# First five attention steps written in another order: inverse sums leave ahead of the transposes, operands split one step sooner, one more piece of w_in converted

## The chip, the core and the metric

The kernel runs on one core of a Trainium2 chip. The metric is the device time of one execution in microseconds (us). A core has a matrix engine (PE, its weight loads shown as PEld), a vector engine (DVE), a scalar engine (ACT), a general engine (POOL) and a queue engine (SP), which here issues every transfer. Each engine runs its own instruction list in order and waits on semaphores for the others; the transfers of SP's queue start in the order written, each once its own waits are over.

## The reference, cut to what matters

Three layers follow one another, on 4 batches of 576 tokens:

```
scores = q k^T / 8 ; cum = cumsum(max(s, 0)) ; scores += min(-(cum_i - cum_j), 0), causal
attn   = exp(scores - max) / (sum + 1e-9) ;  x = attn v          # 4 x 8 heads of 64
h = gelu(x w_in) ; u, v = halves of h ; v = layernorm(v) g_ln
x = x + (u * (w_sg v + b_sg)) w_out                              # w_in and other weights are float64
theta = x w_theta ; y = w_tok_r (x cos theta) + w_tok_i (x sin theta)
out = (x + y) + max((x + y) w_ch, 0)
```

## The kernel before

Attention works on 16 pairs of heads, one step p for each. All matrix products are split into high and low parts: `kh` is K rounded by ACT, `kl` the rest by POOL, `qh` Q/8 rounded by POOL, `ql` the rest by DVE. A step holds, for its pair p: `scores(p, 0)` and `scores(p, 1)` on PE (tiles `sc`, two groups of row blocks that share the same PSUM banks); `reduced` on DVE (adds the bias `C`, takes minimum and maximum, writes `E` and `negm`); `expo` on ACT (exponential, with row sums `sm`); and, for the pair before, `inverse` (DVE: `sm` + 1e-9, then the reciprocal into `r`), seven groups of transposes of `E` on PE (tiles `T`, copied to `Ef` and `E0` by ACT and DVE), and `load_r`. For the pair two before, `values` multiplies by v (tiles `Y`, `Z`), and DVE multiplies the result with `xT`, which holds the inverse sums.

The inverse sums travel: `r` is transposed on PE into a tile `T`, ACT copies it to `rT`, SP stores that to `rd` in HBM, and `load_r` loads `rd` back, spread over partitions, as `xT`. SP cannot issue that load before the store has landed, and whatever stands behind the load in SP's queue waits with it.

The float64 weight `w_in` comes in 8 pieces: `load_piece(k)` (SP, into one of two buffers `wraw`), `scale(k)` (ACT, `wtab` from `wraw`), `bits(k)` (three DVE instructions on `wtab`), `part32(k)` (ACT `wih`, POOL `wil`). A buffer is free for piece k+2 after `bits(k)`.

Up to step 4 (`FIXED = 5`) the order on every engine is the order in which the program text is written (`fixed()` chains it). From step 5 on a scheduler orders the instructions and weaves the first layer after attention (`ffn`, tiles `fo`) into the steps; there the table `PLAN` says which piece is converted (C) or loaded (L) at which of a step's four places (G, H, B: the same for `w_sg` and two vectors). The first half of `ffn_in` needs the pieces 0 to 3, the second half (`fo<-x,wih`) the pieces 4 to 7.

Of the kernel before, what the change touches and what calls it, by code (L numbers as in the profile page):

```python
# [9 lines left out]
F32 = mybir.dt.float32  # L10
# [4 lines left out]
ALU = mybir.AluOpType  # L15
# [24 lines left out]
HALF = [(0, 288), (288, 288)]  # L40
# [15 lines left out]
class Kernel:  # L56
# [12 lines left out]

    PLAN = {5: ("C4 L6", "C5 L7", "C6 G0", "C7 G1 B"), 6: ("H0 G2", "H1 G3", "H2 G4", "H3 G5"),  # L70
# [102 lines left out]
    def begin(self, es):  # L173

        nc = self.nc
        c = self.cp
        p = self.pool(es, "cum")
# [57 lines left out]
        cpos = p.tile([32, S], F32, name="cpos")  # L235
# [3 lines left out]
        os = []  # L239
# [10 lines left out]
        def part(i):  # L250
            a, n = HALF[i]
            cs = slice(a, a + n)
            nc.scalar.copy(ch[:, cs], os[i][0:32, 0:n])
            nc.vector.tensor_copy(cpos[:, cs], os[i][0:32, 0:n])
            nc.sync.dma_start(self.cd[:, cs], cpos[:, cs])
            nc.vector.tensor_tensor(cl[:, cs], cpos[:, cs], f32(ch[:, cs]), op=ALU.subtract)

        def spread(i, j):

            a, n = HALF[i]  # L260
            cs = slice(a, a + n)
            o = ps.tile([P, 512], F32, name="spread", **(
                dict(tag="spread", bufs=2) if i == 0 else dict(tag=f"cumo{HALF[j][0]}")))
# [9 lines left out]
        self.split_k()  # L273
        for f in copies:
            f()
        self.scores(0, 0)
        for j in (0, 1):
            spread(1, j)()
        self.load_pair(1)

# [14 lines left out]
    def attention_pools(self, es):  # L295
# [130 lines left out]
    def transposes(self, pr, kind, j, pool=None):  # L426
# [12 lines left out]
        if kind == "a" and not j:  # L439
            nc.tensor.transpose(T[:, 256:384], self.st[pr % 2][1], self.ident)  # L440
        if kind != "d":
# [4 lines left out]
        def away():  # L446
            if kind == "b":
                nc.vector.tensor_copy(Ef[:, 512:1024], T)  # L448
            elif kind == "c":
                nc.scalar.copy(Ef[:, 0:512], T)  # L450
            elif kind == "d":
                nc.vector.tensor_copy(E0[:, 0:512], T)
            else:
                nc.scalar.copy(Ef[:, 1024:1280], T[:, 0:256])
                if j == 0:
                    rT = self.a1.tile([10, P], F32, name="rT")
                    nc.scalar.copy(rT, T[0:10, 256:384])
                    nc.sync.dma_start(self.rd[pr].rearrange("j (c n) -> (j c) n", c=5), rT)
                else:
                    nc.scalar.copy(E0[:, 512:576], T[:, 256:320])  # L460
        return away

    def transposed(self, pr):
# [79 lines left out]
    def split_k(self):  # L543
        K = self.raw.pop(("K", 0))
        qh, ql, kh, kl = self.ops[0]
        self.rnd("act", kh, K)
        for a, n in HALF:
            self.sub("pool", kl[:, a:a + n], K[:, a:a + n], kh[:, a:a + n])

    def first_steps(self):  # L550

        nc = self.nc
        one = (0, 1)
        for p in range(self.FIXED):
            V = None
            if p:
                self.scores(p, 0)

            Q, K = self.raw["Q", p + 1], self.raw.pop(("K", p + 1))
            qh, ql, kh, kl = self.operands(p + 1)  # L560
            if p:
                self.load_cum(p + 1)
                self.rnd("act", kh, K)
            nc.gpsimd.tensor_scalar(qh, Q, 0.125, 1.0, op0=ALU.mult, op1=ALU.mult)
            if p == 0:
                self.spin(self.psT.tile([P, 512], F32, name="spin", tag="T"), 8)
            else:
                self.sub("pool", kl, K, kh)
            for j in one:
                self.reduced(p, (1, 0, 4), (j,))  # L570
                self.expo(p, (1, 0, 4), (j,))
                if p == 0 and j == 0:
                    self.rnd("act", kh, K)
                    self.sub("pool", kl, K, kh)
                    self.load_cum(1)
            if p:
                self.inverse(p - 1)
            if p > 1:
                V = self.values(p - 2)
            elif p:  # L580
                self.spin(self.psT.tile([P, 512], F32, name="spin", tag="T"), 10)
            self.split_q(p + 1)
            if p:
                self.scale(p - 1)
            self.load_pair(p + 2, "K")
            self.load_pair(p + 2, "Q")
            self.load_v(p)
            self.scores(p, 1)
            if V:
                V("pool")  # L590
            if p == 0:
                self.load_piece(0)
                for t in (3, 2):
                    self.reduced(0, (t,))
                    self.expo(0, (t,))
                self.aux()
                del self.cums[0]
                self.load_piece(1)
                self.spin(self.psT.tile([P, 512], F32, name="spin", tag="T"), 12)
                continue  # L600
            g = p - 1
            a0 = self.transposes(g, "a", 0)
# [25 lines left out]
        self.inverse(self.FIXED - 1)  # L628

    def attention(self):  # L630
# [466 lines left out]
    def run(self):  # L1097
        nc = self.nc
        with ExitStack() as root, ExitStack() as right2, ExitStack() as left2:
# [10 lines left out]
            with self.fixed():  # L1110
# [11 lines left out]
                self.attention_psum(aps)  # L1122
                self.first_steps()
            with aps:
# [137 lines left out]
```

## Time and profile before

| what | us |
|---|---|
| median of 3 runs (lowest, highest) | 666.54 (666.25, 667.63) |
| the profiled execution, its own time | 668.43 |
| its span, first to last instruction | 666.7 |
| PE busy in the span | 630.3 (95%) |
| DVE, ACT, POOL busy | 427.8, 357.0, 178.5 |

The span is what the trace shows; 1.73 us of the profiled execution lie around it. PE is busy 95% of the span, so the idle time of PE, 36 us in all, and the stretches in which its clock is granted only in part are where time can come from; the rows further down show where they lie. The waits are read from the timeline of an engine, where the bracket behind a row gives how long the engine stood idle ahead of it and what ended that.

### The profile page before, as it was taken

To read this page: it belongs to the slowest core of one execution; us is meant where nothing else is said; L and a number is where in the kernel's file an instruction comes from. 1 tells how busy PE (TensorE), PEld (TensorE's weight loads), DVE (VectorE), ACT (ScalarE), POOL (GpSimd) and SP (SyncE) were. 2 spreads that over 40 slices of the span, in tenths; PEclk is the share of its full clock that TensorE was granted. 3 is DMA by queue.
4 is the path that set the end of the run, shared out by engine and by line. 5 is a ranking of instruction groups with operands and counts; after the bars stand their busy time and mean duration, and the time that the engine had idled before them with its cause. 6 is when DMAs were issued, how large, how long until landed. Compare 5 with 4: busy or idle time off the path is not lost.

```text
span 666.7 us, 12668 instructions
## 1 busy us (share of the span) xinstructions
PE 630.3 (95%) x4719; PEld 551.4 (83%) x4719; DVE 427.8 (64%) x1049; ACT 357.0 (54%) x833; POOL 178.5 (27%) x207
## 2 busy tenths in 40 slices
PE   8888869989999999999997799999999999999997
PEld 6666657768877888778787789899999999989997
DVE  6798567757387563863269977787772577468422
ACT  5876548784587744874265335566550454255100
POOL 4344423333205332044396633120000100100000
PEclk9899898999999999999999889999999999999999
DMA  4677554445632565201355789721002100300101
GB/s 121 213 256 240 161 166 145 122 134 179 222 104 88 154 195 187 69 19 73 137 147 179 248 261 363 250 90 55 1 1 88 56 1 36 107 0 2 72 1 72
DMA packets 49806, 83.57 MB, mean 125 GB/s; under 512 B 7921, under 2 KB 19793, under 8 KB 49745
## 3 DMA queue, kind: packets, MB, share of 16 engines
q1 hardware_dynamic: 49744, 82.76, 38.5%
q8 instruction: 37, 0.61, 0.4%
q14 instruction: 25, 0.20, 0.1%
HBM read 61.61 MB, written 21.13 MB: 124 GB/s over the span
## 4 chain that ended last, share of the span: by engine, by line
PE 66%; DMA 9%; DVE 8%; ACT 7%; POOL 5%; issue 3%; SPq 1%; DVEq 0%; ACTq 0%; POOLq 0%
PE yo L109 17%; PE fo L109 13%; PE th L109 8%; PE co L109 8%; PE wo L109 6%; PE Y L109 5%; PE sc L109 5%; PE T L438 3%; DMA wraw<-in_moe_w_in 3%; ACT E L408 2%; DMA rd<-rT 2%; POOL vT L851 2%; DVE E L397 2%; PE tp L1000 1%; DMA xT<-rd 1%
## 5 line engine op out<-in xcount | busy, mean ns | idle before, releaser
L408 ACT ACTIVATE E<-E,negm 128x192 f32<-128x192 f32 (+4 forms) x160 | 88.2, 553 | 1.7 <-DVE negm L397 1.6
L109 PE MATMUL yo<-wkh,zh 128*128 128x288 f32 x288 | 85.2, 296 | 0.2 <-DVE x2T L1073 0.2
L109 PE MATMUL yo<-wkl,zh 128*128 128x288 f32 x288 | 85.2, 296 | 0.0
L109 PE MATMUL yo<-wkh,zl 128*128 128x288 f32 x288 | 85.2, 296 | 0.0
L397 DVE CUSTOM_DVE_ANT_0 E<-sc,C 128x192 f32<-128x192 f32 (+4 forms) x160 | 68.5, 483 | 6.6 <-PE sc L109 6.4
L438 PE MATMUL T<-ident,E 128*128 128x128 f32 x400 | 57.6, 279 | 13.1 <-DVE xT L500 4.9
L109 PE MATMUL fo<-x,wih 128*128 128x288 f32 x256 | 57.3, 306 | 6.1 <-ACT vT L891 3.7
L438 PEld LDWEIGHTS T<-ident,E 128*128 128x128 f32 x400 | 46.4, 142 | 17.8 <-DVE Ef L448 6.0
L109 PEld LDWEIGHTS yo<-wkh,zh 128*128 128x128 f32 x288 | 54.0, 188 | 0.7 <-DVE x2T L1073 0.4
L109 PEld LDWEIGHTS yo<-wkl,zh 128*128 128x128 f32 x288 | 54.1, 188 | 0.3
L109 PEld LDWEIGHTS yo<-wkh,zl 128*128 128x128 f32 x288 | 54.0, 188 | 0.1
L109 PE MATMUL co<-u,wch 128*128 128x288 f32 x256 | 53.0, 295 | 0.0
L102 POOL TENSOR_SCALAR xt<-x2s 128x128 fp32r<-128x128 f32 x16 | 10.8, 691 | 156.1 <-DVE x2s L106 156.1
L109 PEld LDWEIGHTS fo<-x,wih 128*128 128x128 f32 x256 | 42.1, 189 | 8.6 <-ACT vT L891 3.9
L109 PE MATMUL wo<-gh,woh 128*128 128x288 f32 x128 | 39.2, 309 | 7.0 <-ACT gh L98 3.7
L109 PE MATMUL fo<-wih,x 128*128 128x512 f32 x128 | 43.7, 413 | 0.0
L109 PE MATMUL th<-wth,x2s 128*128 128x512 f32 x128 | 42.9, 400 | 0.0
L448 DVE COPY Ef<-T 128x512 f32<-128x512 f32 x32 | 21.6, 685 | 32.9 <-PE T L438 32.5
L98 ACT CAST u<-x2T 128x576 fp32r<-128x576 f32 x16 | 10.8, 672 | 59.3 <-DVE x2T L1073 59.3
L109 PEld LDWEIGHTS co<-u,wch 128*128 128x128 f32 x256 | 41.6, 188 | 0.0
L109 PE MATMUL sc<-kh,qh 64*128 64x288 f32 (+1 forms) x192 | 39.3, 374 | 0.4
L109 PE MATMUL wo<-gl,woh 128*128 128x288 f32 x128 | 37.7, 308 | 1.3 <-DVE gl L106 1.3
(203 smaller groups left out, 1767.3 us busy)
## 6 DMA issues: line engine op xcount, KB each, us to landing
C<-cd SPq DMA_DIRECT2D x15, 576.0 KB, 4.1
Q<-in_q SPq DMA_DIRECT2D x16, 288.0 KB, 3.4
K<-in_k SPq DMA_DIRECT2D x16, 288.0 KB, 3.4
xT<-rd SPq DMA_DIRECT2D x32, 144.0 KB, 3.2
xd<-xT SPq DMA_DIRECT2D x16, 288.0 KB, 2.1
gd<-uT SPq DMA_DIRECT2D x16, 288.0 KB, 2.1
gr<-gd SPq DMA_DIRECT2D x16, 288.0 KB, 3.5
xr<-xd SPq DMA_DIRECT2D x16, 288.0 KB, 4.2
```

The lines of the kernel that those rows point to most:

```text
L98: nc.scalar.copy(out, src)
L102: nc.gpsimd.tensor_scalar(out, src, 1.0, 1.0, op0=ALU.mult, op1=ALU.mult)
L109: return self.nc.tensor.matmul(out, lhsT, rhs, start=start, stop=stop)
L397: self.nc.vector.tensor_tensor_reduce(at if j else at[:, ::-1], self.sc[t, j].rearrange("p (b k) -> p b k", k=64), C[:, j, 0:n].rearrange( ...
L408: self.nc.scalar.activation(at, at, AF.Exp, bias=self.negm[pr % 2][:, j, c:c + 1], scale=-1.0, accum_out=sm[:, j * 5 + c:j * 5 + c + 1])
L438: nc.tensor.transpose(T[:, col:col + P], E[:, c:c + P], self.ident)
L448: nc.vector.tensor_copy(Ef[:, 512:1024], T)
L851: nc.gpsimd.tensor_scalar(vT[0:r, t], vT[0:r, t], rs[0:r, t:t + 1], nm[0:r, t:t + 1], op0=ALU.mult, op1=ALU.add)
L1000: nc.tensor.transpose(tp[0:r, dt * P:(dt + 1) * P], x2T[:, dt, a:a + r], self.ident)
```

## The change

Seven things are different, all in the first five steps and the text around them:

- The start: `kh`, `qh`, `ql` and `kl` of pair 0 stand ahead of the copies of the cumulated sums (`part`), all four `spread` products stand behind `scores(0, 0)`, and the loads of pair 1 are issued among them.
- `load_piece(0)` and `load_piece(1)` stand in step 0 ahead of the loads of pair 2; piece 0 is converted in step 0, piece p in step p, so pieces 0 to 4 are done in the fixed part and `load_piece` goes up to 6. `PLAN` loses C4 and L6.
- `high(p + 2)` (`qh`, `kh`, `kl`) stands at the end of step p, ahead of `part32(p)`; before, it stood in step p + 1 behind `part32(p)`.
- `inverse(p - 1)` stands between the two halves of `reduced(p, (1, 0, 4))`, and `turned` (transpose of `r`, copy to `rT`, store) ahead of `scores(p, 1)`; before, it was part of the first transposes.
- K(p+2) is loaded before `inverse`, Q(p+2) after `low_q`; `load_v` and `load_cum` stand ahead of them.
- Step 1 has 8 spin products (idle work on PE) instead of 10.
- SP, too, now has to keep its later transfers behind the last one written before `values(3)`.

```diff
-    PLAN = {5: ("C4 L6", "C5 L7", "C6 G0", "C7 G1 B"), ...
+    PLAN = {5: ("C5 L7", "C6", "G0", "C7 G1 B"), ...
...
-        self.split_start()
+        Q, K = self.raw.pop(("Q", 0)), self.raw.pop(("K", 0))
+        qh, ql, kh, kl = self.operands(0)
+        nc.gpsimd.tensor_scalar(qh, Q, 0.125, 1.0, op0=ALU.mult, op1=ALU.mult)
+        self.rnd("act", kh, K)
+        self.low_q(0, Q)
+        self.load_pair(1, "Q")
+        for a, n in HALF:
+            self.sub("pool", kl[:, a:a + n], K[:, a:a + n], kh[:, a:a + n])
         part(0)
-        self.split_q(0)
-        copies = [spread(0, 0), spread(0, 1)]
+        self.load_pair(1, "K")
         part(1)
...
+    def high(self, pr):
+        K = self.raw.pop(("K", pr))
+        qh, ql, kh, kl = self.operands(pr)
+        self.nc.gpsimd.tensor_scalar(qh, self.raw["Q", pr], 0.125, 1.0, op0=ALU.mult, op1=ALU.mult)
         self.rnd("act", kh, K)
+        self.sub("pool", kl, K, kh)
...
+        self.load_piece(0)
+        self.load_cum(1)
...
+        self.load_piece(1)
+        self.load_pair(2, "Q")
+        self.load_pair(2, "K")
+        self.load_v(0)
+        self.scale(0)
...
+        self.bits(0)
+        self.load_piece(2)
+        self.high(2)
+        self.part32(0)
+        self.spin(self.psT.tile([P, 512], F32, name="spin", tag="T"), 12)
+        for p in range(1, self.FIXED):
+            g = p - 1
+            self.scores(p, 0)
+            self.load_cum(p + 1)
+            self.load_v(p)
+            self.load_pair(p + 2, "K")
+            self.reduced(p, (1, 0, 4), (0,))
+            self.expo(p, (1, 0, 4), (0,))
+            self.inverse(g)
+            self.reduced(p, (1, 0, 4), (1,))
+            self.expo(p, (1, 0, 4), (1,))
+            self.low_q(p + 1, self.raw.pop(("Q", p + 1)))
+            self.load_pair(p + 2, "Q")
...
+            self.turned(g, self.psF.tile([P, 512], F32, name="T", tag="fo"))
+            self.scores(p, 1)
             if p > 1:
+                away("pool")
+            self.scale(p)
...
-            self.bits(p - 1)
-            self.part32(p - 1)
-            self.load_piece(p + 1)
+            self.bits(p)
+            self.load_piece(p + 2)
+            if p + 2 <= self.FIXED:
+                self.high(p + 2)
+            self.part32(p)
...
         for e, i in self.ends.items():
-            if e != mybir.EngineType.SP:
-                behind.enter_context(self.tc.issue_after(i))
+            behind.enter_context(self.tc.issue_after(i))
```

SP's queue in step 2 of the kernel before, from the load of `C` for pair 3 to the piece of `w_in` (`rd<-rT` stores the inverse sums of pair 1, `xT<-rd` loads them back):

```order
L324 DMA C_584<-cd_60 128x1152
L320 DMA K_619<-in_k 128x576
L320 DMA Q_621<-in_q 128x576
L335 DMA v02_76<-in_v 64x64 x2
L336 DMA vr_623<-in_v 128x4x128
L514 DMA xd_57<-xT_534 128x576
L458 DMA rd_62<-rT_679 10x128
L477 DMA xT_711<-rd_62 64x576 x2
L704 DMA wraw_278<-in_moe_w_in 128x1024
```

The same stretch now:

```order
L328 DMA C_593<-cd_60 128x1152
L339 DMA v02_76<-in_v 64x64 x2
L340 DMA vr_595<-in_v 128x4x128
L324 DMA K_599<-in_k 128x576
L324 DMA Q_616<-in_q 128x576
L470 DMA rd_62<-rT_634 10x128
L523 DMA xd_57<-xT_540 128x576
L486 DMA xT_718<-rd_62 64x576 x2
L705 DMA wraw_278<-in_moe_w_in 128x1024
```

The store of the inverse sums has moved ahead of the store `xd`, which waits for the result of `values`; K and Q have moved behind v.

DVE in step 2 before: the two halves of `reduced` for the two heads, then `inverse`, then `ql` of the next pair (`negm0_77` alone is the read of an accumulator):

```order
L397 ISA E_579,negm0_77<-sc_543,C_418 128x9x64
L397 ISA negm0_77 128x1
L397 ISA E_579,negm0_77<-sc_544,C_418 128x192
L397 ISA negm0_77 128x1
L397 ISA E_579,negm0_77<-sc_544,C_418 128x64
L397 ISA negm0_77 128x1
L397 ISA E_579,negm0_77<-sc_544,C_418 128x576
L397 ISA negm0_77 128x1
L413 TENSOR_SCALAR sm1_81<-sm1_81 128x10
L414 RECIPROCAL r1_82<-sm1_81 128x10
L541 SCALAR_TENSOR_TENSOR ql_581<-Q_452,qh_580 128x576
```

and now:

```order
L401 ISA E_592,negm0_77<-sc_556,C_428 128x9x64
L401 ISA negm0_77 128x1
L417 TENSOR_SCALAR sm1_81<-sm1_81 128x10
L418 RECIPROCAL r1_82<-sm1_81 128x10
L401 ISA E_592,negm0_77<-sc_557,C_428 128x192
L401 ISA negm0_77 128x1
L401 ISA E_592,negm0_77<-sc_557,C_428 128x64
L401 ISA negm0_77 128x1
L401 ISA E_592,negm0_77<-sc_557,C_428 128x576
L401 ISA negm0_77 128x1
L542 SCALAR_TENSOR_TENSOR ql_548<-Q_451,qh_547 128x576
```

`inverse` has moved ahead of the second head's three reductions. ACT around the end of step 0 before (the `E` rows are exponentials, `sm_79` the sums of step 0):

```order
L408 ACTIVATE E,sm_79<-E,negm_77 128x576
L408 ACTIVATE E,sm_79<-E,negm_77 128x448 x2
L408 ACTIVATE E,sm_79<-E,negm_77 128x320 x2
L98 CAST kh<-K 128x576
L408 ACTIVATE E,sm_81<-E,negm_78 128x192
```

and now (`wtab` is `scale`, `wih` is `part32`):

```order
L412 ACTIVATE E,sm_79<-E,negm_77 128x576
L710 ACTIVATE wtab<-wraw 128x512
L412 ACTIVATE E,sm_79<-E,negm_77 128x448 x2
L412 ACTIVATE E,sm_79<-E,negm_77 128x320 x2
L98 CAST kh<-K 128x576
L98 CAST wih<-wtab 128x512
L412 ACTIVATE E,sm_81<-E,negm_78 128x192
```

`scale(0)` now stands in step 0, between the exponentials of the first and of the second group, and `wih` of piece 0 ahead of step 1's exponentials.

## Rows read from the trace of the kernel before

**Rows 1.** Windows: length, busy PE, PEld, DVE, ACT, POOL, PE clock, DMA share, GB/s.
```profile
17.80:30.00 12.20, 9.88 (x93) 8.11 (x94) 9.69 (x29) 9.40 (x30) 2.70 (x3) 0.86 0.78 244
30.00:41.30 11.30, 10.03 (x106) 7.38 (x108) 9.74 (x31) 8.51 (x28) 5.06 (x6) 1.00 0.71 230
...
52.40:63.80 11.40, 9.68 (x78) 6.12 (x80) 11.07 (x32) 9.29 (x29) 5.71 (x6) 1.00 0.73 225
63.80:70.00 6.20, 3.61 (x52) 2.90 (x48) 0.22 (x2) 0.62 (x1) 1.27 (x1) 1.00 0.78 246
70.00:74.00 4.00, 3.93 (x13) 3.20 (x14) 3.19 (x16) 3.09 (x9) 2.19 (x3) 0.57 0.37 147
...
92.40:105.50 13.10, 8.10 (x47) 6.27 (x47) 9.34 (x29) 9.45 (x24) 2.56 (x2) 0.74 0.21 71
105.50:667.00 561.50, 540.96 (x3968) 484.25 (x3967) 351.81 (x814) 286.82 (x628) 138.54 (x153) 0.99 0.35 114
```

**Rows 2.** Waits of PE up to 110 us: total, times, longest.
```profile
PE fo L109 <- ACT vT L891: 3.7, 1, 3.7
PE T L438 <- DVE xT L500: 3.7, 4, 2.7
```

**Rows 3.** Timeline of the start on SP, POOL and DVE: start, us, instruction, [idle before].
```profile
1.83 0.57 SPq L320 DMA_DIRECT2D Q<-in_q  x1
2.45 0.43 SPq L320 DMA_DIRECT2D K<-in_k  x1
...
4.82 0.68 POOL L536 TENSOR_SCALAR qh<-Q 128x576 fp32r<-128x576 f32 x1 [0.51 <-DMA Q<-in_q]
7.54 1.83 POOL L106 TENSOR_TENSOR kl<-K,kh 128x288 fp32r<-128x288 f32 x2 [2.04 <-ACT kh L98]
...
11.24 0.76 DVE L397 CUSTOM_DVE_ANT_0 E<-sc,C 128x576 f32<-128x576 f32 x1 [0.27 <-ACT C L266]
...
17.82 0.36 DVE L397 CUSTOM_DVE_ANT_0 E<-sc,C 128x192 f32<-128x192 f32 x1 [1.84 <-PE sc L109]
```

**Rows 4.** Timeline of ACT in step 1: the first piece of w_in.
```profile
23.97 0.66 ACT L709 ACTIVATE wtab<-wraw 128x512 f32<-128x512 f32 x1 [2.02 <-DMA wraw<-in_moe_w_in]
```

**Rows 5.** Timeline of POOL and DVE: one `kl` and four DVE instructions.
```profile
20.03 1.13 DVE L413 TENSOR_SCALAR sm<-sm 128x10 f32<-128x10 f32 x1
...
32.86 0.71 DVE L541 SCALAR_TENSOR_TENSOR ql<-Q,qh 128x576 fp32r<-128x576 f32 x1
...
44.03 1.41 POOL L106 TENSOR_TENSOR kl<-K,kh 128x576 fp32r<-128x576 f32 x1
44.26 1.81 DVE L541 SCALAR_TENSOR_TENSOR ql<-Q,qh 128x576 fp32r<-128x576 f32 x1
...
70.80 0.16 DVE L413 TENSOR_SCALAR sm<-sm 128x10 f32<-128x10 f32 x1
```

**Rows 6.** Timeline of SP and DVE: the way of the inverse sums.
```profile
25.07 0.35 SPq L458 DMA_DIRECT2D rd<-rT  x1
31.22 1.10 SPq L477 DMA_DIRECT2D xT<-rd  x2
...
34.84 0.23 DVE L500 TENSOR_TENSOR xT<-Z,xT 128x64 f32<-128x64 f32 x1 [1.27 <-PE sc L109]
...
61.35 0.46 SPq L458 DMA_DIRECT2D rd<-rT  x1
65.09 1.10 SPq L477 DMA_DIRECT2D xT<-rd  x2
...
69.79 0.22 DVE L500 TENSOR_TENSOR xT<-Z,xT 128x64 f32<-128x64 f32 x1 [5.98 <-DMA xT<-rd]
```

**Rows 7.** Timeline of SP and ACT in step 5: the last pieces of w_in.
```profile
79.47 0.33 SPq L704 DMA_DIRECT2D wraw<-in_moe_w_in  x1
88.53 0.36 SPq L704 DMA_DIRECT2D wraw<-in_moe_w_in  x1
...
94.35 0.66 ACT L680 ACTIVATE wtab<-wraw 128x512 f32<-128x512 f32 x1 [6.94 <-DMA wraw<-in_moe_w_in]
```

More of the change, by code (lines that the diff above doesn't have):

```diff
@@ L266, in spread @@
             return lambda: nc.scalar.copy(C[:, j, cs], o[:, 0:n])
-        self.split_start()
+        Q, K = self.raw.pop(("Q", 0)), self.raw.pop(("K", 0))
[6 more added lines that the diff above has]
+            self.sub("pool", kl[:, a:a + n], K[:, a:a + n], kh[:, a:a + n])
         part(0)
-        self.split_q(0)
-        copies = [spread(0, 0), spread(0, 1)]
+        self.load_pair(1, "K")
         part(1)
-        self.split_k()
-        for f in copies:
-            f()
         self.scores(0, 0)
         for j in (0, 1):
-            spread(1, j)()
-        self.load_pair(1)
+            for i in (0, 1):
+                spread(i, j)()
         for v in self.v0:
@@ L438, in transposes @@
             nc.tensor.transpose(T[:, col:col + P], E[:, c:c + P], self.ident)
-        if kind == "a" and not j:
-            nc.tensor.transpose(T[:, 256:384], self.st[pr % 2][1], self.ident)
+        if kind == "a" and not j and not pool and pr not in self.turns:
+            self.turned(pr, T)
         if kind != "d":
@@ L454, in away, with turned @@
                 nc.scalar.copy(Ef[:, 1024:1280], T[:, 0:256])
[L455 to L459, printed above, removed]
+                if j:
                     nc.scalar.copy(E0[:, 512:576], T[:, 256:320])
         return away
+    def turned(self, pr, T):
+        nc = self.nc
+        self.turns.add(pr)
+        nc.tensor.transpose(T[:, 256:384], self.st[pr % 2][1], self.ident)
+        rT = self.a1.tile([10, P], F32, name="rT")
+        nc.scalar.copy(rT, T[0:10, 256:384])
+        nc.sync.dma_start(self.rd[pr].rearrange("j (c n) -> (j c) n", c=5), rT)
     def transposed(self, pr):
@@ L546, in split_k @@
         self.rnd("act", kh, K)
-        for a, n in HALF:
-            self.sub("pool", kl[:, a:a + n], K[:, a:a + n], kh[:, a:a + n])
+        self.sub("pool", kl, K, kh)
     def first_steps(self):
[L552 to L565, printed above, removed]
-                self.spin(self.psT.tile([P, 512], F32, name="spin", tag="T"), 8)
[L567 to L577, printed above, removed]
-            if p > 1:
[L579 to L601, printed above, removed]
@@ new lines, in first_steps @@
+        self.load_piece(0)
+        self.load_cum(1)
+        self.spin(self.psT.tile([P, 512], F32, name="spin", tag="T"), 8)
+        for j in (0, 1):
+            self.reduced(0, (1, 0, 4), (j,))
+            self.expo(0, (1, 0, 4), (j,))
+            if j == 0:
+                self.high(1)
+        self.low_q(1, self.raw.pop(("Q", 1)))
+        self.scores(0, 1)
+        self.load_piece(1)
[3 more added lines that the diff above has]
+        self.scale(0)
@@ new lines, in first_steps @@
+        for t in (3, 2):
+            self.reduced(0, (t,))
+            self.expo(0, (t,))
+        del self.cums[0]
+        self.aux()
+        self.bits(0)
[16 more added lines that the diff above has]
+            self.load_pair(p + 2, "Q")
+            if p > 1:
+                away = self.values(p - 2)
+            else:
+                self.spin(self.psT.tile([P, 512], F32, name="spin", tag="T"), 8)
+            self.turned(g, self.psF.tile([P, 512], F32, name="T", tag="fo"))
+            self.scores(p, 1)
+            if p > 1:
+                away("pool")
+            self.scale(p)
@@ L622, in first_steps @@
             self.load_r(g)
-            self.bits(p - 1)
-            self.part32(p - 1)
-            self.load_piece(p + 1)
+            self.bits(p)
[3 more added lines that the diff above has]
+            self.part32(p)
+        queued = next(i for i in reversed(self.nc.cur_bb.bb.instructions) if i.engine == mybir.EngineType.SP)
         self.values(self.FIXED - 2)("act")
         self.inverse(self.FIXED - 1)
+        return queued
     def attention(self):
@@ L1122, in run @@
                 self.attention_psum(aps)
-                self.first_steps()
+                queued = self.first_steps()
+            self.ends[mybir.EngineType.SP] = queued
             with aps:
```

19 lines of the change are left out of this document (5 added, 14 removed).

## The prediction

> **What bounds the kernel now.** I read first the busy shares by stage, then what PE waits for, then the timelines of the engines named there. From 105.5 us to the end PE is busy 541 of 561.5 us at a clock of 0.99 [rows 1]: that part has no room, the change barely touches its order, and it will simply begin earlier or later. The room is in the first 105.5 us. Steps 2 to 4 take 11.3, 11.1 and 11.4 us (the windows, the middle one alike and not shown), with DVE busy for 9.7 to 11.1 of them and PE for 9.7 to 10.0 [rows 1]: DVE sets the pace there and PE is close behind. Three stretches wait for a transfer instead: step 1, where ACT stands 2.02 us for the first piece of w_in [rows 4]; 63.8 to 70, where DVE stands 5.98 us for the inverse sums of pair 3 [rows 6] and PE 2.7 us behind it [rows 2]; and 92.4 to 105.5, where ACT stands 6.94 us for the last piece of w_in [rows 7], PE 3.7 us for ACT's next copy [rows 2], and the clock falls to 0.74 on average [rows 1].
>
> **The change, part by part.**
>
> The start. `kl` of pair 0 began at 7.54 because `kh` stood behind two copies on ACT. Q was issued at 1.83 and read at 4.82, 3.0 us later; K, issued at 2.45, should be there at 5.45, `kh` takes some 0.6, so `kl` begins near 6.1, 1.4 us earlier [rows 3], and the scores with it. All four `spread` products now follow the scores, about 1 us of PE, and ACT's copies of them end near 10.5; the third reduction, which needs two, begins near 9.95 where it began at 11.24 [rows 3]: 1.3 us earlier. Step 1's first reduction at 17.82 waits for scores that wait for the last reductions of step 0 [rows 3], so it moves by the same 1.3. `bits(0)` is new there, three DVE instructions of 1.8 us, and lies in the 1.84 us in which DVE waits for PE [rows 3]; if piece 0 lands later than about 14 us that cover is gone and up to 1 us returns. Taken: -1.3; bounds 0 and -1.8.
>
> Step 1. Piece 0 is converted by then and piece 1 was issued near 10, so ACT's wait of 2.02 [rows 4] goes: 12.2 us become about 10.2. What is late next is `ql`, or `kh` of pair 2 (below). Taken: -2.0; bounds -0.5 and -2.3.
>
> Steps 2 to 4. A `ql` that begins while POOL runs `kl` takes 1.81 us and ends after it; alone it takes 0.71. The add of `inverse`, 0.16 alone, took 1.13 under another `kl` [rows 5]. Now `kl` of pair p+1 runs at the very start of step p, right behind the last `bits`, and `part32`'s POOL half behind it; `ql` comes about 3.1 us into the step, behind both, so its 1.1 us go in steps 3 and 4, while the add, moved ahead, meets the end of `kl` and pays some 0.6, between its 0.16 and its 1.13. In step 2 `ql` was free already and the step loses 1.27 to its `xT` [rows 6], of which half should stay, since step 2 itself comes earlier. Taken: -0.7, -0.9 and -1.1, together -2.7, which leaves steps of 10.2 us, just above PE's 10.0; bounds 0 and -3.6.
> The Trainium skill (SBUF — State Buffer, "SBUF: two separate sides") calls the port pair that the two engines share an exclusive lock, held for a whole instruction. By that rule the change moves the stall from `ql` to the add as much as it removes it, and if the order on POOL slips by half a microsecond both pay; it speaks against this part, and would make it 0. The trace agrees with the lock [rows 5], not with the slip.
>
> The inverse sums of pair 3. The store left at 61.35, the load at 65.09, and DVE had them at 69.79 [rows 6], 17.4 us after the step's start at 52.4. Now the transpose of `r` stands ahead of `scores(p, 1)`, and the store no longer behind `xd`: DVE's second head ends 3.1 us into the step, its exponentials and `rT` a microsecond later, so the store leaves about 4.2 in; it takes 3.7 and the load 4.7 as before [rows 6], which makes 12.6. The step ends 10.2 in, so a wait of 2.4 is left where 5.98 stood. In front of the store stand the loads of K and Q, and Q waits for `ql`; that costs nothing while `ql` (about 3.8 in) ends before `rT`. The rows of PE behind it follow DVE [rows 2]. Taken: -3.6; bounds -1.5 and -5.5.
>
> The clock behind it. From 70 to 74 PE ran at 0.57 [rows 1] after standing 2.7 us [rows 2]. Without the gap these 4 us hold 2.3 us of work, but `x` of pair 3 also has to pass ACT and POOL there. Taken: -1.0; bounds 0 and -1.7.
>
> The last pieces. Piece 7 was issued at 88.53, 9 us after piece 6 at 79.47 [rows 7], since its buffer is freed by piece 5, and C5 stood at the second place of step 5. Now C5 stands at the first, where C4 was: piece 7 takes the place of the issue at 79.47, 9 us earlier against its stage. ACT comes to it at 87.4, its last work ahead of the wait (94.35 less 6.94), and 79.47 plus the 5.8 us that the transfer took is 85.3: the wait of 6.94 goes altogether. PE loses the 3.7 and most of the half-speed clock behind it (13.1 us at 0.74 hold 8.1 busy us, about 5 at full speed). ACT is the engine that has no pause after this, so its share counts: -6.3, allowing 0.6 for a conversion that ends late; bounds -3.5 and -8.
>
> New waits. K and Q of pair 2 now stand behind two pieces of w_in (512 KB each) in SP's queue, and `kh` of pair 2 stands on ACT ahead of step 1's exponentials. At the 230 to 250 GB/s of these stages [rows 1] one piece is 2.1 us. If K lands at 18 and not 17, ACT enters step 1 late by a microsecond, `kl` slides under `ql` or the add, and step 2 inherits it; the PE product of `r` then also waits, and behind a pause of 1 to 2 us the clock of step 2's scores may stay low, as it did (0.86 in this window [rows 1]). No row shows it, so between 0 and 4 I take 1.2, since the nearest row, ACT's wait for a piece, is 2.02 [rows 4] and comes here with half a chance or so.
>
> Sum: -1.3 - 2.0 - 2.7 - 3.6 - 1.0 - 6.3 + 1.2 = -15.7. The profiled execution took 668.43 with a span of 666.7; it becomes 652.7. It lies 1.9 us above the median of three, 666.54, so the forecast is 650.8. A ceiling: of the first 105.5 us PE is busy for 89.3 (630.3 in the span less 541.0 after it [rows 1]), some 6 of them added by the low clock, so no order of this work saves more than about 22.
>
> **Rivals.**
> *The steps give nothing back.* The lock only changes victims and PE, at 10.0 busy us of 11.1 [rows 1], is bound by its copies of `T`; start, step 1 and steps 2 to 4 give 2 instead of 6. For it: DVE and PE are nearly level. Against: `ql`'s 1.1 us are no one's cover. The sum is 11.7, the time 654.8.
> *The sums are as late as before.* The store now stands behind a Q load, which waits for DVE; if Q's buffer is freed late, the store slips by its 4 us, and the clock's microsecond goes with it: the sum is 11.1, the time 655.4. Against: `ql` comes earlier than it did.
> *More than the sum.* The K of pair 2 lands in time, the clock holds from step 1 on, and the last stage falls to PE's own 5 us: no new wait, 1.7 more in the last pieces, 1.5 more in the first steps: 20.1, the time 646.4.
> *Nothing changes:* the time is returned later, where step 6 waits for w_sg and both tables of ACT; then 666.5. Against: these waits are counted from the loads of the same steps and move with them.
> *Slower.* PE works through its list in order, and the transpose of `r` now stands ahead of `scores(p, 1)`. It needs the last exponentials of the step before, and ACT is busy for 9.3 us of a step [rows 1] with `kh`, `wih` and `scale` moved around them. If `r` comes later than `Z` in each of the steps 1 to 4, PE pauses four times, and each pause brings the lower clock level (1.2 instead of 2.4 GHz), as 70 to 74 shows [rows 1]. It decides from two steps on: each such step holds some 10 busy us of PE [rows 1] and takes 10 more at the lower level; with the sums, the clock and the last pieces kept (10.9) and the rest lost, two steps make 666.5 - 10.9 + 20 = 675.6. Against: by the order `r` is ready 2.1 us into the step and `Y` alone ends later.
>
> **How the numbers follow.** Forecast 0.57; steps give nothing 0.16; sums late 0.08; more 0.12; nothing 0.03; slower 0.04. Within 0.2%, 1.3 us, a measurement of this kernel can tell no change: faster 0.93, same 0.03, slower 0.04. The bounds of the terms add to far more than they would together; the range 644 to 658.5 holds the forecast with the four largest terms off by half their distance to the bounds, and the first three rivals.
>
> **What would show it.** Right: the first `kl` near 6.1; step 1's first reduction near 16.5; no wait of ACT for a piece of w_in; `ql` at 0.7 us and the add at 0.5 or more in the steps; steps of 10.2 us; the store of pair 3's sums about 4.5 us into step 4 and DVE's wait for `xT` under 3; piece 7 issued near 69 and no gap of PE near 80; the clock at 1.00 from step 2 to 105; the work from 105.5 on as long as it was. Wrong: a wait for K of pair 2 of over 2 us, PE waiting for `r` in each step, or a stage after 90 us that is longer than its counterpart.

## The result, and the profile after

The changed kernel takes 656.91 us (median of four runs, 654.58 to 659.43) where the kernel before takes 667.09 (four runs, 666.25 to 667.81): the ratio is 0.985, with a 95% interval of 0.981 to 0.989. The profiled execution took 656.72 us, with a span of 655.0 where 666.7 stood. The change is faster, as forecast, by less than forecast: 11.7 us of span in place of 15.7, and the median lies 6.1 us above the 650.8 of the forecast. Of these 6.1 us, 4.0 are in the span; the other 2.1 come from the step from the profiled execution to the median, since that execution lay 1.9 us above its median before and lies 0.2 below it now.

The windows of the changed kernel by stage, with the columns of [rows 1]:

```profile
18.60:32.70 14.10, 10.94 (x82) 9.34 (x84) 8.89 (x29) 10.15 (x31) 4.69 (x5) 0.64 0.61 204
32.70:43.05 10.35, 10.09 (x106) 7.36 (x108) 10.09 (x31) 8.53 (x28) 5.03 (x6) 1.00 0.71 234
...
53.66:63.65 9.99, 9.33 (x78) 5.96 (x76) 9.72 (x32) 8.64 (x29) 5.04 (x5) 1.00 0.74 250
...
87.50:96.00 8.50, 8.50 (x73) 6.22 (x73) 6.69 (x25) 7.75 (x21) 0.15 (x1) 1.00 0.29 86
96.00:655.00 559.00, 539.22 (x3947) 483.93 (x3943) 350.61 (x813) 285.85 (x627) 138.00 (x153) 0.99 0.35 114
```

Read against [rows 1]: the steps are near 10.3 us where they took 11.3, the stage at 0.74 of the clock ahead of 105.5 is now a stage of 8.5 us in which PE never rests, and the long stage behind it is what it was. One stage went the other way: step 1, the first row, now takes 14.1 us, and its granted clock of 0.64 says that PE spent most of it at the lower level. By landmarks of the two traces:

| stretch | before | after | moved | forecast |
|---|---|---|---|---|
| to step 2's first reduction (DVE) | 30.03 | 32.70 | +2.67 | -2.1 (start, step 1, new waits) |
| steps 2 to 4, to the wait for `xT` of pair 3 | 33.78 | 30.93 | -2.85 | -2.7 |
| that wait | 5.98 | 2.23 | -3.75 | -3.6 |
| from there to `Z` of pair 4 (PE) | 38.74 | 30.34 | -8.40 | -7.3 (clock, last pieces) |
| from there to the end | 558.17 | 558.80 | +0.63 | 0 |

So the miss of 4.0 us lies in the first row, +4.8; the second to fourth rows give 1.4 back, and the last adds 0.6. This is what happens there, in the timelines of SP, POOL, ACT, PE and DVE (in this order), to be read against [rows 3] and [rows 4]:

```profile
11.29 0.33 SPq L328 DMA_DIRECT2D C<-cd  x1
11.66 0.43 SPq L705 DMA_DIRECT2D wraw<-in_moe_w_in  x1
12.90 0.33 SPq L324 DMA_DIRECT2D Q<-in_q  x1
14.51 0.33 SPq L324 DMA_DIRECT2D K<-in_k  x1
...
6.28 1.56 POOL L106 TENSOR_TENSOR kl<-K,kh 128x288 fp32r<-128x288 f32 x2 [0.68 <-ACT kh L98]
...
20.99 0.68 POOL L548 TENSOR_SCALAR qh<-Q 128x576 fp32r<-128x576 f32 x1 [6.50 <-DMA Q<-in_q]
...
21.71 0.67 ACT L98 CAST kh<-K 128x576 fp32r<-128x576 f32 x1 [4.23 <-POOL qh L548]
...
20.16 0.33 PE L467 MATMUL T<-ident,r 128*128 128x128 f32 x1 [2.29 <-DVE r L418]
...
26.17 3.46 PE L442 MATMUL T<-ident,E 128*128 128x128 f32 x15 [1.59 <-ACT rT L469]
...
18.58 0.36 DVE L401 CUSTOM_DVE_ANT_0 E<-sc,C 128x192 f32<-128x192 f32 x1 [1.58 <-DMA C<-cd]
...
32.70 0.36 DVE L401 CUSTOM_DVE_ANT_0 E<-sc,C 128x192 f32<-128x192 f32 x1 [1.41 <-PE sc L109]
```

The start did come earlier (`kl` at 6.28, where 7.54 stood). But Q of pair 2, issued at 12.90 behind C of pair 1 and piece 1, is not read before 20.99, 8.1 us later. ACT has `kh` of pair 2 at the head of its list and stands 4.23 us for K, issued at 14.51. (The row names POOL's `qh`, which ended at about the moment K came; in b1 and c4 the row of `kh` names the load of K, and in b4 `kh` begins at 19.63, before `qh`, 19.50 to 20.18, has ended.) Step 1's exponentials, `rT` and the transposes follow late. PE stands for `r` (itself late, since step 1's first reduction waited 1.58 us for C), then 1.59 us for `rT`.

The parts that came as forecast, from POOL, DVE, SP, PE and ACT, against [rows 5], [rows 6] and [rows 7]:

```profile
43.45 1.41 POOL L106 TENSOR_TENSOR kl<-K,kh 128x576 fp32r<-128x576 f32 x1 [2.05 <-ACT kh L98]
...
44.15 0.74 DVE L417 TENSOR_SCALAR sm<-sm 128x10 f32<-128x10 f32 x1
...
46.10 0.76 DVE L542 SCALAR_TENSOR_TENSOR ql<-Q,qh 128x576 fp32r<-128x576 f32 x1
...
57.97 0.32 SPq L470 DMA_DIRECT2D rd<-rT  x1
...
62.24 1.10 SPq L486 DMA_DIRECT2D xT<-rd  x2
...
75.27 0.33 SPq L705 DMA_DIRECT2D wraw<-in_moe_w_in  x1
...
64.97 0.31 PE L109 MATMUL Z<-E,v 128*64 128x64 f32 x4
...
65.86 0.23 DVE L509 TENSOR_TENSOR xT<-Z,xT 128x64 f32<-128x64 f32 x1 [2.23 <-DMA xT<-rd]
...
82.79 0.69 ACT L681 ACTIVATE wtab<-wraw 128x512 f32<-128x512 f32 x1
```

`ql` takes 0.76 us in each step, the add 0.87, 0.74 and 0.43; the store of pair 3's sums leaves 4.3 us into step 4, and of the 2.23 us that DVE still stands ahead of `xT` the last 0.6 alone belong to the sums, since PE ends `Z` of that pair at 65.28; ACT's conversion of piece 7 has no wait in its brackets, where 6.94 us stood.

### The profile page after: what moved, and what is told of

Read it like the earlier page. It is cut to its first block, busy times and chain, and to the rows that moved or that the text cites. A ratio compares the mean times of both kernels' runs of the same rounds, so it can differ in the third digit from the quotient of the medians.

```text
span 655.0 us, 12671 instructions
## 1 busy us (share of the span) xinstructions
PE 628.3 (96%) x4717; PEld 551.1 (84%) x4717; DVE 424.0 (65%) x1049; ACT 356.8 (54%) x833; POOL 177.8 (27%) x207
## 4 chain that ended last, share of the span: by engine, by line
PE 74%; DVE 9%; ACT 8%; DMA 3%; POOL 3%; issue 2%; SPq 0%; DVEq 0%; POOLq 0%; ACTq 0%
PE yo L109 17%; PE fo L109 16%; PE th L109 8%; PE co L109 8%; PE wo L109 8%; PE T L442 5%; PE sc L109 5%; PE Y L109 5%; ACT E L412 3%; DVE E L401 2%; PE tp L1001 1%; DMA Q<-in_q 1%; POOL vT L852 1%; ACT vT L900 1%; DVE stats L843 1%
## 5 line engine op out<-in xcount | busy, mean ns | idle before, releaser
L442 PE MATMUL T<-ident,E 128*128 128x128 f32 x400 | 59.1, 286 | 5.1 <-DVE Ef L452 2.0
L442 PEld LDWEIGHTS T<-ident,E 128*128 128x128 f32 x400 | 48.2, 146 | 9.4 <-DVE Ef L452 3.4
L109 PE MATMUL fo<-wsh,vh 128*128 128x288 f32 x128 | 38.9, 308 | 1.6 <-ACT wsh L98 1.6
L951 POOL TENSOR_TENSOR uT<-gt,uT 128x288 f32<-128x288 f32 x32 | 27.7, 870 | 45.3 <-DVE gt L949 43.9
```

The lines of the kernel that those rows point to most:

```text
L109: return self.nc.tensor.matmul(out, lhsT, rhs, start=start, stop=stop)
L951: nc.gpsimd.tensor_tensor(uT[:, ft, a:a + m], gt, uT[:, ft, a:a + m], op=ALU.mult)
```

## The experiments

Twelve kernels ran beside the kernel before (667.68, 666.82 and 667.44 us in the three groups a, b and c). Columns: the start of step 2's first reduction; steps 2 to 4; DVE's wait ahead of `xT` of pair 3 (for the sums, or for PE's `Z` of the pair, whichever is later); from there to `Z` of pair 4; the rest of the span, all from one profile each; then the median of all runs and its ratio to before with the interval. The first five columns add up to the span.

| kernel | step 2 | 2 to 4 | wait | to Z | rest | median | ratio |
|---|---|---|---|---|---|---|---|
| before | 30.03 | 33.78 | 5.98 | 38.74 | 558.17 | 667.09 | 1 |
| changed | 32.70 | 30.93 | 2.23 | 30.34 | 558.80 | 656.91 | 0.985 [0.981, 0.989] |
| a1 changed again | 29.60 | 30.93 | 5.04 | 29.34 | 560.09 | 657.05 | 0.986 [0.983, 0.989] |
| a2 piece 1 later | 29.11 | 31.82 | 2.96 | 29.62 | 558.29 | 655.63 | 0.982 [0.980, 0.985] |
| a3 26 spins | 31.06 | 31.30 | 2.84 | 29.74 | 558.96 | 656.81 | 0.986 [0.983, 0.989] |
| a4 pieces as before | 27.56 | 32.71 | 3.61 | 39.42 | 560.50 | 665.18 | 0.997 [0.994, 0.999] |
| b1 transpose of `r` back | 31.79 | 31.35 | 5.72 | 29.36 | 560.18 | 659.01 | 0.987 [0.985, 0.990] |
| b2 high parts back | 28.90 | 33.49 | 2.16 | 30.42 | 559.23 | 655.89 | 0.984 [0.981, 0.987] |
| b3 a2, store by ACT | 27.41 | 31.25 | 2.27 | 30.32 | 561.65 | 655.34 | 0.982 [0.980, 0.985] |
| b4 a2, high(2) in step 1 | 28.07 | 32.87 | 4.58 | 29.33 | 557.85 | 655.44 | 0.983 [0.980, 0.986] |
| c1 pieces behind | 27.71 | 31.30 | 1.71 | 30.87 | 558.11 | 652.29 | 0.977 [0.975, 0.980] |
| c2 c1 and b4 | 27.71 | 31.64 | 1.73 | 30.84 | 559.18 | 652.79 | 0.978 [0.975, 0.980] |
| c3 a2, no store awaited | 27.58 | 33.09 | 3.82 | 29.31 | 560.60 | 655.05 | 0.980 [0.978, 0.983] |
| c4 SP not held | 32.02 | 30.77 | 2.76 | 29.84 | 559.31 | 656.92 | 0.983 [0.980, 0.986] |

### a1: the changed kernel again

No edit.

> The changed kernel once more, beside the variants below: 656.9 us (654.6 to 659.4 in its first four runs), 10 us below before. Its trace put the whole gain behind 33 us: step 2 began at 32.7 where it began at 30.0.

Measured: the same time, another way there. In the timelines of ACT and DVE:

```profile
19.70 0.68 ACT L98 CAST kh<-K 128x576 fp32r<-128x576 f32 x1 [2.09 <-POOL qh L548]
...
65.57 0.23 DVE L509 TENSOR_TENSOR xT<-Z,xT 128x64 f32<-128x64 f32 x1 [5.04 <-DMA xT<-rd]
```

`kh` of pair 2 comes 2.0 us earlier than in the first profile and step 2 3.1 us earlier; the wait for pair 3's sums grows by 2.8 and both spans are 655.0. The store of these sums left 5.6 us into step 4 here and its load followed 5.9 us behind it, where both were 4.3 in the first profile. So the landing times of step 1's loads differ from execution to execution, and what one stretch gains the next wait can take back. A difference of 3 us in one stretch of one profile is not yet an effect of an edit.

### a2 and a3: piece 1 later, and PE kept busy

```diff
-        self.load_piece(1)
         self.load_pair(2, "Q")
         self.load_pair(2, "K")
         self.load_v(0)
+        self.load_piece(1)
```

> Theory A (the queue): K and Q of pair 2 stand behind two pieces of w_in; with the second piece behind them they land about 2 us earlier (512 KB at some 300 GB/s), ACT's wait of 4.2 us for K becomes about 2.3, step 2 begins near 30.7 instead of 32.7 and the time is about 655 us. Theory B (the load of C for pair 1 alone is late): it still lands at 18.5, step 2 begins where it did, 656.9. Theory C (the clock of PE alone, after it waited for r): the wait for r stays, step 2 begins where it did, 656.9.

Measured, in the timeline of ACT:

```profile
18.88 0.68 ACT L98 CAST kh<-K 128x576 fp32r<-128x576 f32 x1 [1.26 <-DMA K<-in_k]
```

ACT's wait is 1.26 us, and step 2 comes at 29.11. The median falls by 1.4 us against a1 on the same chip, less than the two intervals tell apart. The second kernel leaves the loads alone and gives PE 26 idle products in place of 8 ahead of the transpose of `r` in step 1:

```diff
-                self.spin(self.psT.tile([P, 512], F32, name="spin", tag="T"), 8)
+                self.spin(self.psT.tile([P, 512], F32, name="spin", tag="T"), 26)
```

> 26 idle products instead of 8 ahead of the transpose of r in step 1, so that PE does not stand there. Theory C (the clock): the granted clock stays at 1.00 up to 24 us or longer, the 15 transposes and the scores of step 2 take 1.8 and 1.9 us instead of 3.5 and 3.1, step 2 begins near 30.4 and the time is about 654.6. Theory A: ACT's wait for K of pair 2 stays at 4.2 us; what the clock gives back is hidden behind ACT up to the copy of rT at 25.9, so step 2 begins at best near 31.5, 656. If the clock falls all the same behind ACT's lateness: 656.9.

Measured, in the timeline of PE:

```profile
25.24 0.66 PE L442 MATMUL T<-ident,E 128*128 128x128 f32 x4 [2.54 <-ACT rT L469]
```

PE no longer stands for `r`, but still 2.54 us for `rT`; the clock of the stage is 0.87 (a1 had 0.86 without the extra products); step 2 at 31.06 and the time, 656.81, are within the spread of the changed kernel. So the pause for `r` alone is not what costs: without it PE still waits for ACT. What a clock kept at 1.00 would give is not shown here, since the products did not keep it there.

### a4: the pieces of w_in loaded and converted as before

```diff
-    PLAN = {5: ("C5 L7", "C6", "G0", "C7 G1 B"),
+    PLAN = {5: ("C4 L6", "C5 L7", "C6 G0", "C7 G1 B"),
...
-            self.scale(p)
+            self.scale(p - 1)
...
-            self.load_piece(p + 2)
+            self.load_piece(p + 1)
```

(`bits`, `part32` and the first loads likewise one step later.)

> The pieces of w_in as before the change (loaded at the end of step 0, converted one step later, C4 and L6 in the table), all else as changed. Theory A: K and Q of pair 2 land near 17, ACT's wait for K is under 1 us, step 1 begins near 17 and step 2 near 28 to 29; the last piece is late again, ACT waits some 7 us for it and PE 4, which costs 7 to 8: 656.9 - 4 + 7.5, about 660. Theory B: step 1 still waits for C and step 2 begins near 31.5 or later: 663 or more.

Measured: 665.18 us, 8 of the 10 us gone. The early gains are all there, and larger: step 2 at 27.56 with the clock at 1.00 through step 1. But from pair 3's `xT` to `Z` of pair 4 it is 39.42 us again (38.74 before, 29.3 to 30.9 in every kernel with the new pieces), and ACT stands as it did in [rows 7]:

```profile
87.24 0.66 ACT L677 ACTIVATE wtab<-wraw 128x512 f32<-128x512 f32 x1 [6.05 <-DMA wraw<-in_moe_w_in]
```

This undoes one part alone and so shows both of its sides: the pieces bring some 9 us behind 66 us, and cost in step 1.

### b1: the transpose of r inside the transposes again

```diff
-            self.turned(g, self.psF.tile([P, 512], F32, name="T", tag="fo"))
```

> The changed kernel, with r of the inverse sums transposed inside the first transposes of the step again, behind scores(p, 1), as before the change. Theory (the early transpose is what brings pair 3's sums forward): the store of pair 3's sums leaves about 3 us later in step 4, DVE's wait for xT grows from 2.2 us to about 5.5 to 6, and the time rises by 3 to 4 us, to about 660.5. Rival (the sums come earlier only because the steps are shorter): the wait stays near 2 to 3 us and the time near 657. A second effect of the other sign belongs to both: in step 1 PE no longer stands 2.3 us for r and 1.6 us for rT, so step 2 can begin 1 to 2 us earlier than in the changed kernel; if that is passed on, the time is 658.5 to 659.5 in the first case and about 655.5 in the rival.

Measured, in the timeline of ACT in step 1 (the first row) and those of ACT, SP and DVE in step 4:

```profile
21.60 0.67 ACT L98 CAST kh<-K 128x576 fp32r<-128x576 f32 x1 [3.96 <-DMA K<-in_k]
...
57.49 0.26 ACT L469 COPY rT<-T 10x128 f32<-10x128 f32 x1
...
58.64 0.56 SPq L523 DMA_DIRECT2D xd<-xT  x1
60.24 0.30 SPq L470 DMA_DIRECT2D rd<-rT  x1
...
68.86 0.22 DVE L509 TENSOR_TENSOR xT<-Z,xT 128x64 f32<-128x64 f32 x1 [5.72 <-DMA xT<-rd]
```

The store stands behind `xd` again and leaves 8.1 us into the step (52.19) in place of 4.3, and the wait is 5.72 us, near the 5.98 of before: the theory's number. Counted from the start of step 4, DVE had the sums 16.7 us in, where it was 12.2 in the changed kernel and 17.4 before. With the transpose early that figure is up to 15.4 in other profiles (b4; 15.3 in a1), so one profile of each shows the direction better than the size. The median rises by 2 us, to 659.01; its interval overlaps that of the changed kernel, so the trace shows the 3.5 us and the time only a part. PE does not wait for `r` here, yet step 2 comes at 31.79, since ACT stood 3.96 us for K of pair 2: once more ACT, and not the pause for `r`.

### b2: the high parts at the start of the step again

```diff
-        self.high(2)
...
             self.load_cum(p + 1)
+            self.high(p + 1)
...
-            if p + 2 <= self.FIXED:
-                self.high(p + 2)
```

> The changed kernel, with the high parts of K and Q of pair p+1 taken at the start of step p again, ahead of its first reduction, and not at the end of step p-1. Theory (the shorter steps come from ql's free port): ql takes 1.8 us in steps 2 to 4 in place of 0.75, the add of the inverse sums is back near 0.2 to 0.6 in place of 0.4 to 0.9, and each of steps 3 and 4 is 0.6 to 1.0 us longer than 10.6 and 10.0, the time 1.5 to 2.5 us longer, about 659. Rival (the stall only changes victims, and the steps are shorter for their order on PE): steps 2 to 4 last 30.9 us as in the changed kernel and the time stays at 657, or falls by up to 1 us since ACT's wait for K of pair 2 stands in step 1 at the same place.

Measured: steps 2 to 4 take 33.49 us in place of 30.93, nearly the 33.78 of before. Step 3 on DVE:

```profile
41.17 1.03 DVE L417 TENSOR_SCALAR sm<-sm 128x10 f32<-128x10 f32 x1
...
43.41 1.40 DVE L542 SCALAR_TENSOR_TENSOR ql<-Q,qh 128x576 fp32r<-128x576 f32 x1
```

Both pay here, the add 1.03 and `ql` 1.40, against 0.74 and 0.76. So the theory holds in the rows of the steps. The time doesn't show it: the median, 655.89, is no longer than the changed kernel's. In this profile step 2 came early and the wait for `xT` of pair 3 was 2.16 us, the shortest of groups a and b.

### b3 and b4: the store in a queue of its own, and ACT freed of K

Both have piece 1 later, as a2. The first lets ACT issue the store of the sums:

```diff
-        nc.sync.dma_start(self.rd[pr].rearrange("j (c n) -> (j c) n", c=5), rT)
+        nc.scalar.dma_start(self.rd[pr].rearrange("j (c n) -> (j c) n", c=5), rT)
```

> The changed kernel with piece 1 of w_in behind Q, K and V of step 0 (655.6 us), and the 5 KB store of the inverse sums issued by ACT right behind its copy rT, in a queue of its own and not behind the loads of K and Q in SP's queue. Theory (the store is late because 1.5 MB of loads stand ahead of it in its queue): it lands about 2 us after its issue in place of nearly 5, the load of xT is issued as soon as SP comes to it, DVE's wait for xT of pair 3 falls from 3.0 us to below 1, and the time falls by 2 to 3 us, to about 653. Rival (queues share the same 16 engines, so the store waits as long in any queue): the wait stays near 3 and the time at 655.6, or 656 with ACT's issue of some 0.3 us in each step.

Measured, in step 4 (ACT's queue, SP, DVE):

```profile
52.61 0.28 ACTq L470 DMA_DIRECT2D rd<-rT  x1
...
57.22 1.10 SPq L486 DMA_DIRECT2D xT<-rd  x2
...
60.93 0.23 DVE L509 TENSOR_TENSOR xT<-Z,xT 128x64 f32<-128x64 f32 x1 [2.27 <-DMA xT<-rd]
```

SP waited for the store's landing and issued the load 4.6 us after the store: a queue of its own didn't make 5 KB land sooner than SP's did (57.97 to 62.24, 4.3 us, in the changed kernel; 4.9 us in a2, whose order of loads it shares). The rival is right. This profile reaches `Z` of pair 4 earlier than any other (91.25 us by the table) and loses 3 us behind it: ACT stands 3.49 us for a load of w_sg at 117.75, and PE 2.83 us for ACT at 123.64. The second kernel takes `kh` of pair 2 behind step 1's first exponentials:

```diff
-        self.high(2)
...
             self.expo(p, (1, 0, 4), (0,))
+            if p == 1:
+                self.high(2)
             self.inverse(g)
```

> The changed kernel with piece 1 of w_in behind Q, K and V of step 0 (655.6 us), and the high parts of pair 2 taken inside step 1, behind its first exponentials, so that ACT doesn't stand for K of pair 2 ahead of them. Theory (ACT's late entry into step 1 delays r, rT and the transposes, and the clock with them): ACT's exponentials of step 1 begin 1 to 2 us earlier, rT comes near 21.5 in place of 23.05, the first reduction of step 2 near 27.5 in place of 29.1, and the time falls by about 1 us, to 654.5; ql of pair 2 may take 1.8 us under kl, which lies in DVE's wait for PE. Rival (what step 2 gains is taken back by the wait for xT of pair 3, whose store and load go at their own pace): step 2 begins earlier, that wait grows by as much, and the time stays at 655.6.

Measured, in the timelines of ACT and DVE:

```profile
21.73 0.24 ACT L469 COPY rT<-T 10x128 f32<-10x128 f32 x1
...
65.52 0.22 DVE L509 TENSOR_TENSOR xT<-Z,xT 128x64 f32<-128x64 f32 x1 [4.58 <-DMA xT<-rd]
```

`rT` and step 2 (28.07) come early as the theory has it, and the wait for pair 3's sums grows as the rival has it. The time, 655.44, is the rival's, but the theory's lies within the spread of the runs too.

### c1 and c2: every piece behind the step's urgent transfers

```diff
-        self.load_piece(1)
         self.load_pair(2, "Q")
         self.load_pair(2, "K")
         self.load_v(0)
+        self.load_piece(1)
...
-        self.load_piece(2)
...
             self.turned(g, self.psF.tile([P, 512], F32, name="T", tag="fo"))
+            self.load_piece(p + 1)
...
-            self.load_piece(p + 2)
+            if p == self.FIXED - 1:
+                self.load_piece(p + 2)
```

> The changed kernel with pieces 1 to 5 of w_in each issued behind K and Q of its step and behind the store of the inverse sums, piece p+1 in step p, and not ahead of them. Theory (the SP queue is full in the steps, about 2.5 MB in 10.5 us, and what stands behind 512 KB lands 2 us later): no wait of ACT for K in steps 1 to 4 over 0.5 us, the store of pair 3's sums lands 3 us after its issue in place of 4.3 to 5.7, DVE's wait for xT of pair 3 is 1 us in place of 3.0, and the first score product of pair 4's end is 2 us earlier than with piece 1 alone moved; the time falls by 1 to 2 us against that kernel's 655.6, to about 654.2. Rival (the store's time comes from its 16 engines being busy with whatever the queue holds, in any order): the wait for xT stays between 2.2 and 5 us and the time at 655.6.

Measured: 652.29 us, a ratio of 0.977 whose interval lies wholly below that of the changed kernel (they ran in different groups, each against the kernel before). In its own group stands c4, which differs from the changed kernel by an edit without effect: 656.92. Against a2 the intervals touch. Step 4, on SP and DVE:

```profile
53.00 0.43 SPq L470 DMA_DIRECT2D rd<-rT  x1
53.48 0.34 SPq L706 DMA_DIRECT2D wraw<-in_moe_w_in  x1
55.82 1.10 SPq L486 DMA_DIRECT2D xT<-rd  x2
...
60.72 0.22 DVE L509 TENSOR_TENSOR xT<-Z,xT 128x64 f32<-128x64 f32 x1 [1.71 <-PE Z L109]
```

The load follows the store after 2.8 us in place of 4.3, and DVE's wait of 1.71 us is no longer for it: the row names PE's `Z`. So the sums are in time although step 4 begins 5 us earlier than in the changed kernel, and step 1 runs at a clock of 1.00, as its window shows (columns of [rows 1]):

```profile
17.40:27.71 10.31, 7.88 (x88) 6.32 (x88) 9.79 (x29) 8.96 (x30) 4.22 (x4) 1.00 0.89 282
```

One sign of the theory failed: ACT still stood 1.35 us for K of pair 2, and step 2 was early all the same. In c1 and c2 alone the sums hold up nobody at the end of step 4. The second kernel adds b4's edit:

> As the kernel with pieces 1 to 5 behind the store, and the high parts of pair 2 taken inside step 1 behind its first exponentials too. Theory (both late operands of step 1 gone): step 2's first reduction near 27.4, the wait for xT of pair 3 as in that kernel, the time 653 to 654.5. Rival (what comes earlier ahead of 66 us is given back at xT of pair 3, and what comes earlier ahead of 100 us at the load of w_sg near 120): 655.4 whatever step 2 does.

Measured: 652.79 us with step 2 at 27.71, as c1. With the loads in order, where `kh` of pair 2 stands makes no difference that can be told.

### c3: no store awaited

With piece 1 later, as a2; pair 3 is divided by the sums of pair 2.

```diff
-    ... self.rd[pr, j:j + 1, 0:S] ...
+    ... self.rd[pr - (pr == self.FIXED - 2), j:j + 1, 0:S] ...
```

> The changed kernel with piece 1 of w_in behind Q, K and V of step 0 (655.6 us), in which pair 3 is divided by the sums of pair 2, which are stored 10 us earlier: its output for pair 3 differs, and no store is waited for. Theory (the wait for pair 3's sums is what takes back the gain of the steps): the load of xT of pair 3 is issued near 56 in place of 60, DVE's wait of 3.0 us is gone, the end of pair 4 comes 2.5 to 3 us earlier, and, if nothing takes it back later, the time is 652.8. Rival (the load of w_sg near 120, on which ACT and then PE stand, has its own pace): of these 3 us half or more is lost at 115 to 127, where PE's wait for wsh or Ef grows from 2.2 to over 3 us, and the time is 654 to 655.6.

Measured: 655.05 us. Neither mechanism is what the trace has (SP, PE, DVE):

```profile
56.68 0.34 SPq L523 DMA_DIRECT2D xd<-xT  x1
58.45 1.10 SPq L486 DMA_DIRECT2D xT<-rd  x2
...
62.02 0.31 PE L109 MATMUL Z<-E,v 128*64 128x64 f32 x4
...
64.49 0.23 DVE L509 TENSOR_TENSOR xT<-Z,xT 128x64 f32<-128x64 f32 x1 [3.82 <-PE sc L109]
```

The row names PE's scores, the last event ahead of it, but DVE needs only `Z`, which was over at 62.33; the load is what is left. It is issued 1.6 us earlier than in a2 (60.05), and DVE begins 0.6 us later than there: 6.0 us after the issue, where a2 took 3.8. PE's wait near 124 us for the converted w_sg, on which the rival rested, was 1.55 us, no longer than the changed kernel's 1.63 (b3 had the longer one). So, by this reading, the wait is not the store's alone: the load can be as late in the crowd of transfers around it.

### c4: SP not held behind the first steps

```diff
-            behind.enter_context(self.tc.issue_after(i))
+            if e != mybir.EngineType.SP:
+                behind.enter_context(self.tc.issue_after(i))
```

> The changed kernel with SP left out of the engines whose instructions of the later part are held behind the first steps, as before the change. Theory (SP's list is the same either way up to the loads of step 5): the same landmarks within the spread of the changed kernel's own runs, and 657. Rival (the held SP delays or protects the loads around 64): piece 7 or the first loads of step 5 are issued 1 us or more earlier or later than 75.3, and the time changes by 1 us or more.

Measured: 656.92 us; piece 7 issued at 74.97 (75.27), step 2 at 32.02, ACT 4.33 us for K of pair 2: the changed kernel in all. This edit is worth nothing that can be measured.

## Why the forecast was right, and where it failed

**Start and step 1.** Half right. `kl` came at 6.28 (6.1 was forecast) and ACT's wait for a piece is gone, but step 1's first reduction is at 18.58 and not 16.5, since C of pair 1 landed late. In the other twelve profiles it is at 17.0 to 18.0, for 17.82 before. The 17.02 of a4, which has no `bits(0)` there and waits 1.82 us for PE's scores, says that the start gave 0.8 us of its 1.3 and that `bits(0)` cost nothing.

**New waits: the step that failed.** The forecast named the place, K and Q of pair 2 behind two pieces of w_in, and the chain from ACT to `r` and the clock, and priced it at 1.2 us, as a wait of 2.02 that "comes here with half a chance or so". It is no matter of chance: ACT stood 4.23, 2.09, 3.27, 3.96 and 4.33 us in the five profiles with piece 1 ahead and `kh` at the head of ACT's list (changed, a1, a3, b1, c4), each time over the 2 us that the forecast itself named as a sign of being wrong. Step 2 began there at 31.4 on average, against 27.9 in the six with piece 1 later (a2, b3, b4, c1, c2, c3, some with other edits too): 3.5 us. 27.9 is 2.1 us ahead of before, where the start and step 1 without new waits were to give 3.3. By these averages those two terms were 1.2 us too large and this one 2.3 too small. In the first profile, whose step 2 was the latest of all, C came late too, and the miss is 4.8 us.

PE's clock is part of the price. Step 1 took 12.1 to 14.7 us in the six profiles in which its granted clock was 0.64 (changed) or 0.86 to 0.88 (a1, a2, a3, b1, c4), and 10.1 to 11.8 in the seven in which it was 1.00. The 11.8 is b2, where ACT stood 2.58 us with the clock at 1.00. How the rest divides between ACT's lateness and the clock is not shown, since both come in the same profiles.

**Steps 2 to 4.** Right in size in the first profile (-2.85 for -2.7) and in cause, by the rows of b2. The sum alone would not show it: kernels that keep this part took 30.8 to 33.1 us (33.09 in c3 and 32.87 in b4, where DVE stood about 1 us for `xT` in two of the steps), and b2's 33.49 is hardly longer. The Trainium skill (SBUF — State Buffer, "SBUF: two separate sides") has the shared ports locked for a whole instruction. The traces agree: the add takes 0.16 us alone and 0.74 where `kl` runs beside it, and it ends as `kl` does, at 44.9. The slip that would have made both `ql` and the add pay didn't come in the changed kernel; in b2 it did.

**The inverse sums.** Right in the first profile (-3.75 for -3.6), with some luck. From the start of step 4 DVE had them after 12.2 us, where the forecast had 12.6, before it was 17.4, and b1 took 16.7. But the second profile of the same kernel (a1) took 15.3, with a wait of 5.04, and b4 15.4, with 4.58. The forecast did not reckon with a chain of store and load that differs by 3 us from profile to profile. It also took the 2.4 us that it left for the load's; in the first profile most of them are PE's `Z`, a floor that it didn't name (1.71 in c1).

**Clock and last pieces.** Right, by -8.4 for -7.3; a4 gives them back. The two terms are not told apart: a4 gives all of it back although its clock, too, is 1.00 from 66 to 87 us. Piece 7 was issued at 75.27 and not near 69, which cost nothing, since ACT came to it at 82.79. By the medians the pieces bear most of the gain: without them 8.1 us are lost (a4 against a1), without the early transpose 2.1 (b1), without the early high parts nothing (b2).

**The rivals.** 656.9 lies nearer to the times of the first two rivals (654.8 and 655.4) than to the forecast, but not for their reasons: the steps gave as much as forecast, the sums did come earlier, and PE paused for `r` in step 1 alone (2.29 us), not in each step. The slower case's mechanism did appear there, a pause and the lower clock behind it. In that profile `r` was late with C of pair 1; in a1 and a3 PE stood 0.60 us and nothing for `r`, then 2.26 and 2.54 for `rT`, which ACT's lateness held up, and the clock fell there too.

**What stays open.** Why the same loads land up to 2 us apart from one execution to the next, and which transfer of the crowd holds the load of c3, was not settled.

## What to carry to other kernels

A bulk load that is moved up in a queue is paid by everything issued behind it: look up who waits first for each of those transfers, and put loads with a whole step of slack behind them; here the same loads in another order (c1) were worth some 4.6 us more. A wait at the end of a step is what its chain (a store, a load) takes less what the step takes: 12.2 us less 10.0 left the 2.2 here, so a shorter step alone makes it longer. Take a second profile of the same kernel before a difference of a few microseconds in one stretch is explained.

## What the runs showed of the hardware

The same program's early loads landed at different times: with K of pair 2 issued at 14.51 and 14.65, ACT read it at 21.71 and 19.70 (changed, a1). A store of 5 KB took 4.6 us to land in a queue of its own (b3) while the 576 KB of K and Q moved in SP's, and 4.3 and 4.9 in SP's queue behind them (changed, a2). With no piece of `w_in` ahead of them either it took 2.8 (c1).
